# Four layers of attention and feed-forward on one core: key weights held behind a select on GpSimd, and a new hand-written order on every engine

## The chip, the core and the metric

The kernel runs on one NeuronCore of a Trainium2 chip. The metric is the device time of one execution in microseconds (us). The kernel before takes 410.4 us in the median of three runs (410.1 to 411.93).

## What is computed

The reference takes x of 2048 tokens by 512 features (bf16) through four layers: linear attention A, feed-forward B, then A and B again with the same weights. Each layer reads the layernorm of x and adds its result to x.

```
A: q, k, v = layernorm(x) @ wqkv               # 32 heads of 16
   phi(t)  = where(t > 0, t + 1, exp(t)) + 1e-6
   kv = sum over tokens of phi(k)^T v ;  z = sum over tokens of phi(k)
   o  = (phi(q) kv) / (phi(q) z + 1e-6) ;  x = x + o @ wo
B: x = x + (silu(layernorm(x) @ w_gate) * (layernorm(x) @ w_up)) @ w_down   # 1792 wide
```

## The kernel before

**Layout.** The 2048 tokens are 16 tiles of 128, in 4 groups of 4 tiles. x stays in SBUF (`X`) from the first load to the last addition. Layers are numbered 0 to 3; 0 and 2 are attention, 1 and 3 feed-forward. All operations are written into one list; each gets the operations that it depends on, and `sync` (line 64) turns these into semaphore waits. What is not computed by the program is the order: `PROGRAM` (line 169) lists TensorE's products as tokens, and `ORDER` (line 193) gives every other engine (ACT is ScalarE, DVE VectorE, POOL GpSimd, SP SyncE, which only issues transfers) its whole sequence by name, written out. An engine takes its list strictly in that order, so an instruction that waits holds up everything behind it. `ON_ACT` (line 328) chooses an engine for each operation that could run on more than one, and `PE_T` (line 322) names the transposes that TensorE does in place of a transposing transfer.

**Tokens.** The first digit is the layer. `S` is a filler product of zeros (`spin`, line 1229). `t` transposes a tile on TensorE (`xt_pe`, line 614), whose copy out of PSUM is `xT`. `k` and `q` are the key product of a tile and the query product of a group and a quarter of the features (lines 662, 766); each is followed by phi (line 642): `exp` on ACT, on some also `id1` on ACT, then `ts` and `phi` on DVE. `g` adds phi(k)^T x-normalized into four PSUM banks that stay taken for the whole pass. `z` adds the key sums of one tile with four one-column products (line 713); tiles of an attention layer without a `z` token are added by `zs` on DVE or POOL (`z_add`, line 703), and one `s` token (`z_sum`, line 725, with `zh` and `zl` on DVE) brings that sum in. `d` is the denominator, `v` and `m` turn the sums into one 512 by 512 matrix (DVE `mask`, then `evac` by ACT or DVE), `r` repeats 1/den on TensorE, `w` is the output product of a tile, with the residual addition `res` on DVE and the next layer's layernorm (`ln`, line 543: `sq` on ACT, `negm`, `vpe`, `pow`, `nmr` mostly on POOL, `apply` on ACT or DVE, then the transposing transfer `xT` from SP's queue). `u` is a gate and an up product (line 873; two PSUM banks, `silu` or `tanh` on ACT, `h` on DVE). `y` and `p` are the seven half-size products of a Strassen step, for gate and up in layer 3 (`gs`, line 978) and for down (`down`, line 1104).

**1/den.** `den` (line 780) takes 1/den in one of two ways: `ln` and then `rex` on ACT (a logarithm and exponentials of its negative), or `den` on DVE (with a reciprocal) and then `rep`, a plain copy, on ACT. Either makes four repeated tiles, each transposed by a transfer (`rT`) and multiplied in by `pqn` on DVE. Each exponential or logarithm is bound to come before each `silu` of the next feed-forward layer, and the reverse (`after=silus`, `after=exps`).

**Head.** SP issues the loads of x tiles 0, 2, 3, 1 and then pairs of tiles, the query and the value weights. ACT's first two instructions are the loads of the key weights (`ldk`, line 500), which wait for nothing. Tiles 0 and 1 get their mean and variance on DVE (`stats`, `aggr`), tiles 2 and 3 on ACT (`stats`, `sq`); tiles 0 to 3 are transposed on TensorE, 3 copied out by DVE and 0, 1 and 2 by ACT. POOL makes the constants; the block mask (`late_consts`, line 478, three operations) comes last among them. POOL issues the loads of the other weights (`ld`) once all x tiles of layer 0 are transposed.

**PSUM.** `bank` (line 430) gives each product the bank of eight that was touched longest ago in the program's order and isn't pinned.

Of the kernel before, what the change touches and what calls it, by code (L numbers as in the profile page):

```python
# [1350 lines left out]
```

## Time and profile before

| | |
|---|---|
| Runs | 410.4 us median (410.1, 410.4, 411.93) |
| Profiled execution | 410.17 us, of which its span is 408.1 |
| TensorE busy | 398.8 us, 98% of the span |
| VectorE busy | 323.8 us, 79% |
| ScalarE busy | 245.3 us, 60% |
| GpSimd busy | 130.4 us, 32% |
| Chain that ended last | TensorE 93%, VectorE 3%, ScalarE 2%, issue 1%, DMA 1% |
| HBM read, written | 9.70 MB, 2.10 MB |

The span runs from the first to the last instruction; the execution's own time has 2.07 us more around it. The chain is followed back from the last instruction, at each step to what released it. Idle time of an engine off the chain costs nothing by itself. In the rows below "x" is a count; a group's us is busy time, its ns the mean of one; in brackets stands the idle time just before and what ended it. Lines are lines of the kernel.

### The profile page before, as it was taken

To read this page: it belongs to the slowest core of one execution; us is meant where nothing else is said; L and a number is where in the kernel's file an instruction comes from. 1 tells how busy PE (TensorE), PEld (TensorE's weight loads), DVE (VectorE), ACT (ScalarE), POOL (GpSimd) and SP (SyncE) were. 2 spreads that over 40 slices of the span, in tenths; PEclk is the share of its full clock that TensorE was granted. 3 is DMA by queue.
4 is the path that set the end of the run, shared out by engine and by line. 5 is a ranking of instruction groups with operands and counts; after the bars stand their busy time and mean duration, and the time that the engine had idled before them with its cause. 6 is when DMAs were issued, how large, how long until landed. Compare 5 with 4: busy or idle time off the path is not lost.

```text
span 408.1 us, 7644 instructions
## 1 busy us (share of the span) xinstructions
PE 398.8 (98%) x2673; PEld 244.8 (60%) x2714; DVE 323.8 (79%) x754; ACT 245.3 (60%) x492; POOL 130.4 (32%) x277
## 2 busy tenths in 40 slices
PE   7999999999999999999999998999999999999997
PEld 6445544444574764445776444444578778878886
DVE  4996488679558978889787957998588788699796
ACT  5998799654417148344166777897773562576440
POOL 5624137772303015000044210698702142030210
PEclk9999999999999999999999999999999999999999
DMA  8757824932201102000011202434210100100011
GB/s 274 139 104 267 200 51 92 194 54 52 51 2 40 14 2 51 0 1 2 2 26 28 52 2 59 80 58 91 51 27 2 43 11 2 51 2 2 0 53 52
DMA packets 53189, 23.30 MB, mean 57 GB/s; under 512 B 46432, under 2 KB 52064, under 8 KB 53152
## 3 DMA queue, kind: packets, MB, share of 16 engines
q1 hardware_dynamic: 51264, 16.27, 18.9%
q0 software_dynamic: 1344, 6.03, 4.7%
q10 hardware_dynamic: 544, 0.52, 0.4%
q8 instruction: 21, 0.34, 0.4%
q14 instruction: 16, 0.13, 0.1%
HBM read 9.70 MB, written 2.10 MB: 29 GB/s over the span
## 4 chain that ended last, share of the span: by engine, by line
PE 93%; DVE 3%; ACT 2%; issue 1%; DMA 1%; SPq 0%; DVEq 0%; ACTq 0%
PE pb L451 93%; DMA X<-in_A_x_dram 1%; DVE X L865 1%; DVE pq L853 1%; DVE GT L743 0%; ACT xnA L571 0%; ACT xnA L563 0%; DVE pq L835 0%; ACT xnT L630 0%; DVE pq L1212 0%; ACT xnB L598 0%; ACT etmp L571 0%; ACT etmp L646 0%; DVE xnA L1142 0%; DVE xnB L602 0%
## 5 line engine op out<-in xcount | busy, mean ns | idle before, releaser
L451 PE MATMUL pb<-xnT,Wu 128*128 128x512 bf16 (+1 forms) x383 | 95.0, 362 | 0.3
L451 PE MATMUL pb<-xnT,Wg 128*128 128x512 bf16 (+1 forms) x370 | 92.4, 362 | 0.9
L451 PEld LDWEIGHTS pb<-xnT,Wu 128*128 128x128 bf16 x388 | 37.9, 98 | 39.4
L451 PEld LDWEIGHTS pb<-xnT,Wg 128*128 128x128 bf16 x388 | 37.8, 98 | 34.5 <-issue 0.5
L899 DVE TENSOR_TENSOR hT<-tht,pb 128x512 bf16<-128x512 f32 x50 | 34.0, 683 | 21.9 <-PE pb L451 14.8
L897 ACT ACTIVATE tht<-pb 128x512 f32<-128x512 f32 x50 | 29.4, 591 | 27.2 <-PE pb L451 26.5
L646 ACT ACTIVATE etmp<-pb 128x512 bf16<-128x512 f32 x64 | 37.0, 597 | 14.1 <-PE pb L451 11.9
L1025 POOL TENSOR_TENSOR hT<-pq 128x256 bf16<-128x256 f32 x24 | 18.5, 775 | 76.7 <-ACT pq L1015 76.7
L575 POOL TENSOR_SCALAR mv<-sums 128x1 f32<-128x1 f32 x52 | 13.6, 270 | 86.4 <-DVE sums L1222 55.0
L888 ACT ACTIVATE tht<-pb 128x512 f32<-128x512 f32 x32 | 19.0, 595 | 35.5 <-PE pb L451 34.4
L451 PE MATMUL pb<-Wd,hT 128*128 128x256 bf16 x336 | 40.1, 273 | 0.0
L1030 ACT ACTIVATE pq<-pb 128x512 f32<-128x512 f32 x45 | 26.0, 595 | 22.3 <-PE pb L451 19.4
L591 POOL TENSOR_TENSOR rstd<-vpe,negh 128x1 f32<-128x1 f32 x62 | 35.8, 582 | 7.8 <-DVE vpe L587 3.0
L451 PEld LDWEIGHTS pb<-Wd,hT 128*128 128x128 bf16 x336 | 32.9, 98 | 5.7
L1020 DVE TENSOR_TENSOR pq<-pb,pq 128x512 f32<-128x512 f32 x45 | 30.2, 685 | 3.6 <-PE pb L451 1.7
L451 PE MATMUL pb<-Wqkv,xnT 128*128 128x512 bf16 x125 | 30.5, 379 | 1.5 <-ACT xnT L630 1.3
L451 PE MATMUL pb<-GT,pq 128*128 128x512 bf16 x125 | 29.9, 379 | 1.5 <-ACT GT L740 1.4
L451 PE MATMUL pb<-xnT,Wqkv 128*128 128x512 bf16 x122 | 30.9, 379 | 0.3
L451 PE MATMUL pb<-pk,xnA 128*128 128x512 bf16 x123 | 30.7, 378 | 0.3
L651 DVE TENSOR_SCALAR etmp<-etmp 128x512 bf16<-128x512 bf16 x64 | 18.4, 291 | 13.7 <-ACT etmp L646 13.5
L890 DVE SCALAR_TENSOR_TENSOR tht<-tht,pb 128x512 f32<-128x512 f32 x32 | 21.8, 684 | 6.1 <-ACT tht L888 5.9
L571 ACT ACTIVATE etmp<-X,sums 128x512 bf16<-128x512 bf16 x32 | 22.8, 715 | 4.5 <-DVE X L865 4.2
(165 smaller groups left out, 724.6 us busy)
## 6 DMA issues: line engine op xcount, KB each, us to landing
out_dram<-pq SPq DMA_DIRECT2D x16, 128.0 KB, 1.7
Wg<-in_B_w_gate_dram POOLq DMA_DIRECT2D x4, 448.0 KB, 5.1
Wu<-in_B_w_up_dram POOLq DMA_DIRECT2D x4, 448.0 KB, 5.5
Wd<-in_B_w_down_dram POOLq DMA_DIRECT2D x7, 256.0 KB, 4.2
X<-in_A_x_dram SPq DMA_DIRECT2D x6, 256.0 KB, 5.3
Wqkv<-in_A_wqkv_dram SPq DMA_DIRECT2D x2, 512.0 KB, 7.4
X<-in_A_x_dram SPq DMA_DIRECT2D x4, 128.0 KB, 3.5
Wqkv<-in_A_wqkv_dram ACTq DMA_DIRECT2D x2, 256.0 KB, 3.8
```

What stands on the lines that cost most here:

```text
L451: return op("pe", lambda e: e.matmul(o_ap, lhsT=lhsT, rhs=rhs, start=start, stop=stop, skip_group_check=skip), r=r, w=w, n=n)
L571: op("act", lambda a: a.activation(out=sq_ap, in_=X[:, t, :], func=ACT.Square, scale=-float(D), bias=sums[:, t:t + 1], accum_out=mv[:, t, ...
L591: op("pool", lambda p: p.tensor_tensor(out=rstd[:, t:t + 1], in0=vpe[:, t:t + 1], in1=negh[:], op=ALU.pow), r=[f"vp{t}", "negh"], w=[f"rs{ ...
L646: exps.append(op("act", lambda a: a.activation(out=etmp[e][:], in_=PB[pb], func=ACT.Exp), r=[f"pb{pb}"], w=[f"e{e}"], after=silus, kind="e ...
L651: op("dve", lambda v: v.tensor_scalar(out=etmp[e][:], in0=etmp[e][:], scalar1=1.0, scalar2=1e-6, op0=ALU.min, op1=ALU.add), r=[f"e{e}"], w ...
L888: op("act", lambda e: e.activation(out=tht[a][:], in_=PB[pg], func=ACT.Tanh, scale=0.5), r=[f"pb{pg}"], w=[f"th{a}"], kind="tanh")
L890: op("dve", lambda v: v.scalar_tensor_tensor(out=tht[a][:], in0=tht[a][:], scalar=1.0, in1=PB[pg], op0=ALU.add, op1=ALU.mult), r=[f"pb{pg} ...
L897: silus.append(op("act", lambda e: e.activation(out=tht[a][:], in_=PB[pg], func=ACT.Silu), r=[f"pb{pg}"], w=[f"th{a}"], after=exps, kind=" ...
L899: op("dve", lambda v: v.tensor_tensor(out=hT[h][:, j, :], in0=tht[a][:], in1=PB[pu], op=ALU.mult), r=[f"pb{pu}", f"th{a}"], w=hk, kind="h")
L1020: op("dve", lambda v: v.tensor_tensor(out=c, in0=PB[b], in1=c, op=ALU.add), r=[f"pb{b}", k], w=[k], kind="ca")
L1025: lambda e: e.tensor_tensor(out=hT[h][:, jj, o:o + 256], in0=c[:, 0:256], in1=c[:, 256:512], op=ALU.mult),
L1030: op("act", lambda e: e.activation(out=gs_tmp[3 * f + n], in_=PB[pb], func=ACT.Copy), r=pk_, w=[f"gt{3 * f + n}"], kind="cp")
```

## The change

**The wait.** The three mask operations move from `late_consts` ahead of the loads, and both loads of the key weights wait for the second of them, the first select on the mask (`begun`). POOL's order of constants becomes: mask memset, identity memset, 1 + 1e-6, first mask select, identity select, and the rest.

```diff
+        op("pool", lambda g: g.memset(mask[:], 1.0), w=["mask"])
+        begun = op("pool", lambda g: g.affine_select(out=mask3, in_=mask3, compare_op=ALU.is_ge, fill=0.0, base=0,
+                                             pattern=[[-DH, HC], [0, DH]], channel_multiplier=1),
+           r=["mask"], w=["mask"])
...
         for c in range(2):
-            dma("act", Wqkv[:, 2 * c:2 * c + 2, D:2 * D], wq3[:, 2 * c:2 * c + 2, D:2 * D], w=[f"Wk{c}"], kind="ldk")
+            dma("act", Wqkv[:, 2 * c:2 * c + 2, D:2 * D], wq3[:, 2 * c:2 * c + 2, D:2 * D], w=[f"Wk{c}"],
+                after=[begun], kind="ldk")
```

**The order.** All tokens of `PROGRAM` and all lists of `ORDER` are new. In tokens, five `z` of layer 0 go and one `s` comes (so the key sums of tiles 6, 8, 10, 11 and 14 go through `zs`), one transpose on TensorE (`2t1`) takes the place of a transfer, and fillers grow from 54 to 60, of which 52 (before: 51) stand ahead of the first transpose. All other products are the same ones. The head, the end of layer 0 and the passage from layer 2 to layer 3:

```diff
-S S S S S S S S S S S S S S S S S S S S S S S S S S S S S S S S S S S S S S S S S S S S S S S S S S S 0t0 S 0k0 S S
-0t2 0t1 0t3 0k2 0k1 0k3 0q00 0q03 0g0 0g2 0g1 0g3 0k4 0k9 0q01 0k10 0k5 0g4 0z2 0g9 0z1 0k6 0z3 0z10 0q12 0k7 0k13
+S S S S S S S S S S S S S S S S S S S S S S S S S S S S S S S S S S S S S S S S S S S S S S S S S S S S 0t0 S S 0t2 S
+S S S S S 0t1 0k0 0k1 0t3 0k2 0k3 0q00 0g1 0g0 0q03 0g2 0k4 0g3 0k9 0q01 0k5 0k10 0g4 0g9 0k6 0k7 0z2 0z5 0z4 0k13
...
-0v 0q31 0m0 0q33 0m2 0m3 0m1 0w1 0w2 0w3 0d30 0r2 0w0 0w5 0q32 0w4 0d31 0w6 0w7 0w11 0d32 0w9 0w8 0w10 1u000 1u007
+0d13 0d01 0d02 0d12 0d03 0g11 0q10 0q20 0g7 0g10 0d10 0d23 0d11 0g15 0g13 0g12 0d21 0q30 0d22 0d20 0v 0q31 0m1 0m3 0m0
+0m2 0q33 0w1 0w2 0d31 0w3 0d30 0r2 0w0 0q32 0w5 0w6 0w7 0w4 0w10 0w9 0w11 0d32 0w8 0d33 1u008 1u004 1u006 1u001 1u000
...
-2d21 2g15 2q23 2d11 2g1 2q22 2g12 2g6 2d13 2d23 2g8 2g5 2d10 2d12 2g4 2d20 2d22 2q33 2v 2r1 2m3 2m1 2m2 2m0 2w3 2w2
-2w0 2q32 2w1 2w6 2d31 2q30 2w4 2w8 2w7 2d32 2w10 2w9 2d33 2w11 2d30 2w5 3u001 3u010 3u004 3u008 3u005 3u000 3u002
+2d23 2d13 2d20 2g6 2g4 2d22 2g1 2q33 2v 2r1 2m3 2m1 2m0 2m2 2w2 2w3 2w0 2q32 2d33 2w1 2d31 2w6 2w4 2q30 2w8 2d32 2w7
+2w9 2w10 2d30 2w5 2w11 3u010 3u012 3u003 3u004 3u008 3u002 3u007 2w15 3u011 3u005 3u009 2w14 2w12 2w13 3u001 3y101
```

**The lists.** The parts that matter below (ACT at the head, at the end of layer 0 and into layer 3; DVE at the head; POOL around the weight loads; SP at the head):

```diff
-i.ldk i.ldk1 0x2.stats 0x2.sq 0x3.stats 0x3.sq 0t0.xT 0k0.exp 0t2.xT 0t1.xT 0k0.id1 0x4.apply 0k2.exp 0k1.exp 0x6.stats 0k3.exp
+i.ldk i.ldk1 0x2.stats 0x2.sq 0x3.stats 0x3.sq 0t1.xT 0k0.id1 0k0.exp 0k1.exp 0x4.apply 0k2.exp 0x6.stats 0x5.apply
...
-0q20.exp 0q20.id1 0d0.rex2 0d1.ln 0G0.evac 0G2.evac 0G3.evac 0d1.rex1 0q30.exp 0d1.rex 0d2.ln 0d2.rxs 0q31.exp
-0M0.evac 0q33.id1 0M1.evac 0M3.evac 0q33.exp 0d1.rex2 0d1.rex3 1x1.sq 1x2.sq 1x3.sq 1x2.apply 1x0.sq 0q32.id1
+0d0.rex2 0q20.exp 0d1.ln 0d1.rex 0d1.rex1 0G0.evac 0G2.evac 0G3.evac 0d1.rex2 0q30.exp 0d2.ln 0d1.rex3 0d2.rxs
+0q31.exp 0M1.evac 0M0.evac 0M3.evac 0q33.id1 0q33.exp 1x1.sq 1x2.sq 1x3.sq 1x2.apply 0q32.id1 1x0.sq 1x5.sq
...
-2d0.rex2 2d1.ln 2d1.rxs 2G2.evac 2G3.evac 2d2.ln 2q33.exp 2q33.id1 2d2.rex 2d2.rex1 2M1.evac 2M0.evac 2M2.evac
-2d2.rex2 3x3.sq 2d2.rex3 3x2.sq 2q32.exp 3x0.sq 3x1.sq 3x6.sq 2q30.exp 3x0.apply 3x4.sq 3x1.apply 3x7.sq 3x8.sq
-3x10.sq 3x9.sq 3x6.apply 3x4.apply 3u001.silu 2d3.rep1 2d3.rep 3u010.silu 3u004.silu 3x7.apply 3x5.sq 3u008.silu
+2G0.evac 2G2.evac 2G3.evac 2q33.exp 2q33.id1 2d2.rep1 2d2.rep3 2d2.rep 2M1.evac 2M0.evac 2M2.evac 2d2.rep2 3x2.sq
+3x3.sq 2q32.exp 3x0.sq 3x1.sq 3x6.sq 2q30.exp 3x0.apply 3x4.sq 3x1.apply 3x8.sq 2d3.ln 3x7.sq 2d3.rex1 2d3.rex
+3x9.sq 3x5.sq 3x10.sq 3x11.sq 2d3.rex3 2d3.rex2 3u010.silu 3u012.silu 3u003.silu 3x8.apply 3u004.silu 3u008.silu
...
-i.c 0x0.stats 0x0.aggr 0x0.apply 0x1.stats 0x2.vpe 0x1.aggr 0x1.vpe 0x3.vpe 0x2.apply 0x4.stats 0x1.apply 0x3.apply
-0x4.aggr 0x9.stats 0x10.stats 0x9.aggr 0t3.xT 0k0.ts 0x5.stats 0k0.phi 0x9.apply 0x10.aggr 0x5.aggr 0k2.ts
+i.c 0x0.stats 0x2.vpe 0x0.aggr 0x1.stats 0x2.apply 0x1.aggr 0x0.apply 0x1.vpe 0x4.stats 0t0.xT 0x1.apply 0x3.vpe
+0x4.aggr 0t2.xT 0x9.stats 0x3.apply 0x9.aggr 0x10.stats 0x5.stats 0t3.xT 0k0.ts 0x5.aggr 0k1.ts 0k0.phi 0k1.phi
...
-i.c5 i.c i.c2 i.c6 i.c1 i.c4 i.c3 i.c7 i.c8 i.c9 0x0.vpe 0x0.pow 0x2.negm 0x3.negm 0x2.pow 0x1.pow 0x3.pow 0x4.vpe
+i.c7 i.c5 i.c2 i.c8 i.c6 i.c i.c1 i.c4 i.c9 i.c3 0x2.negm 0x2.pow 0x0.vpe 0x0.pow 0x3.negm 0x1.pow 0x3.pow 0x4.vpe
...
+0x7.nmr 0x14.negm 0x15.vpe 0x13.vpe 0x15.pow 0x13.pow 0x14.nmr 0x8.vpe 0x8.pow 0x8.nmr 0k10.zs i.ld 0k14.zs i.ld7
...
-i.ldx i.ldx2 i.ldx3 i.ldx1 i.ldy i.ldy2 i.ldy3 i.ldy1 i.ldq i.ldy5 i.ldy4 i.ldv 0x4.xT 0x9.xT 0x10.xT
+i.ldx2 i.ldx i.ldx1 i.ldx3 i.ldy i.ldy2 i.ldy3 i.ldq i.ldy1 i.ldy4 i.ldy5 i.ldv 0x4.xT 0x9.xT 0x5.xT 0x10.xT 0x6.xT
```

**The engines.** By count of instructions in the lists, ACT goes from 433 to 418, DVE from 690 to 707, POOL from 273 to 264. In layer 0 the copies of tiles 0 and 2 after their transposes go to DVE, one more pair of `rsl` and `rse` to ACT. Into layer 2, `2G0` goes to ACT and the way of 1/den changes in groups 1 and 2 (to DVE and `rep`) and in group 3 (to `ln` and `rex`). In layer 3 eight `apply` go from ACT to DVE.

## Rows read from the trace of the kernel before

**Rows 1.** Windows by stage: length, busy PE, PEld, DVE, ACT, POOL, clock, DMA.
```profile
0.00:8.00 8.00, 5.55 (x56) 5.50 (x58) 2.88 (x10) 4.79 (x10) 3.92 (x20) 1.00 0.80 256
8.00:26.00 18.00, 17.69 (x104) 8.53 (x105) 17.96 (x53) 16.29 (x35) 9.96 (x28) 1.00 0.71 154
...
50.00:62.00 12.00, 11.42 (x92) 5.79 (x92) 10.81 (x29) 11.17 (x26) 3.39 (x10) 1.00 0.33 66
62.00:250.00 188.00, 186.93 (x1099) 104.64 (x1118) 147.75 (x356) 99.42 (x190) 52.42 (x112) 1.00 0.19 38
250.00:264.00 14.00, 12.78 (x97) 6.22 (x98) 13.89 (x37) 12.60 (x28) 6.32 (x18) 1.00 0.31 63
264.00:280.00 16.00, 15.87 (x85) 7.38 (x85) 13.75 (x34) 15.35 (x30) 15.47 (x32) 1.00 0.38 73
...
403.00:409.00 6.00, 2.20 (x21) 1.72 (x18) 2.06 (x6) 0.00 (x0) 0.00 (x0) 0.98 0.26 89
```

**Rows 2.** Timeline of the head: start, duration, engine, what, idle before and releaser.
```profile
0.79 3.82 SPq L494 DMA_DIRECT2D X<-in_A_x_dram  x8
0.82 0.97 ACTq L494 DMA_DIRECT2D Wqkv<-in_A_wqkv_dram  x2
...
1.24 5.28 PE L451 MATMUL pb<-hT 128*128 128x128 bf16 x51 [1.24 <-DVE hT L457]
...
1.85 0.35 POOL L481 TENSOR_SCALAR_AFFINE_SELECT mask<-mask 128x128 bf16<-128x128 bf16 x1
...
4.20 0.63 ACT L563 ACTIVATE xnA<-X 128x512 bf16<-128x512 bf16 x1 [2.13 <-DMA X<-in_A_x_dram]
...
6.31 0.69 DVE L556 BATCH_NORM_STATS2 stats<-X 128x6 f32<-128x512 bf16 x1 [0.92 <-DMA X<-in_A_x_dram]
6.36 0.39 PE L625 MATMUL pb<-ident,xnA 128*128 128x128 bf16 x4
...
8.06 0.81 PE L451 MATMUL pb<-Wqkv,xnT 128*128 128x512 bf16 x3 [1.26 <-ACT xnT L630]
...
10.05 2.12 PE L451 MATMUL pb<-Wqkv,xnT 128*128 128x512 bf16 x9
```

**Rows 3.** The same timeline, later: the first two query products.
```profile
12.65 1.89 PE L451 MATMUL pb<-xnT,Wqkv 128*128 128x512 bf16 x8
```

**Rows 4.** Groups of DVE by line and form over the whole span.
```profile
L556 DVE BATCH_NORM_STATS2 stats<-X 128x6 f32<-128x512 bf16 x12 | 8.1, 681 | 2.8 <-DMA X<-in_A_x_dram 2.8
...
L602 DVE TENSOR_SCALAR xnA<-X,mv,rstd 128x512 bf16<-128x512 bf16 x17 | 6.8, 407 | 2.4 <-POOL rstd L591 2.2
...
L633 DVE COPY xnT<-pb 128x512 bf16<-128x512 bf16 x1 | 0.4, 391 | 0.0
```

**Rows 5.** Timeline of PE in layer 0: a z token and the product after it.
```profile
23.01 0.24 PE L451 MATMUL pb<-ones,pk 128*128 128x1 bf16 x4
23.11 1.02 PE L451 MATMUL pb<-pk,xnA 128*128 128x512 bf16 x4
```

**Rows 6.** Timeline of POOL in layer 0: the first weight load.
```profile
31.44 0.98 POOL L494 DMA_DIRECT2D Wo<-in_A_wo_dram  x1 [4.70 <-DMA xnT<-xnA]
```

**Rows 7.** Timelines of PE and ACT at the end of layer 0.
```profile
55.50 2.60 PE L451 MATMUL pb<-GT,pq 128*128 128x512 bf16 x11 [0.47 <-ACT GT L740]
...
54.84 1.09 ACT L740 ACTIVATE GT<-pb 128x512 bf16<-128x512 f32 x2
```

**Rows 8.** Timelines of PE and ACT in the same place of layer 2.
```profile
255.21 2.75 PE L451 MATMUL pb<-GT,pq 128*128 128x512 bf16 x12 [0.90 <-ACT GT L740]
...
253.98 1.57 ACT L740 ACTIVATE GT<-pb 128x512 bf16<-128x512 f32 x3
```

**Rows 9.** Timelines of PE and ACT where layer 3 begins.
```profile
267.70 1.03 PE L451 MATMUL pb<-xnT,Wg 128*128 128x512 bf16 x4
...
269.58 1.28 ACT L897 ACT_TABLE_LOAD   x1
270.87 0.60 ACT L897 ACTIVATE tht<-pb 128x512 f32<-128x512 f32 x1
```

More of the change, by code (lines that the diff above doesn't have):

```diff
@@ L194 @@
     "act": """
-i.ldk i.ldk1 0x2.stats 0x2.sq 0x3.stats 0x3.sq 0t0.xT 0k0.exp 0t2.xT 0t1.xT 0k0.id1 0x4.apply 0k2.exp 0k1.exp 0x6.stats 0k3.exp
-0q00.id1 0q00.exp 0x5.apply 0q03.exp 0x6.sq 0x14.stats 0x14.sq 0x7.apply 0k4.id1 0k4.exp 0k9.exp 0x14.rsl 0q01.exp
-0x14.rse 0k10.id1 0k10.exp 0k5.exp 0x14.apply 0x11.rsl 0x8.apply 0x11.rse 0k6.exp 0q12.id1 0q12.exp 0k7.id1 0k7.exp
-0k13.exp 0k15.exp 0k13.id1 0k14.exp i.c2 i.c1 0q13.exp i.c3 i.c 0q11.exp 0k8.exp 0k8.id1 0k11.id1 0k11.exp 0q02.exp
-0q02.id1 0q23.id1 0k12.exp 0q23.exp 0q22.id1 0q22.exp 0q21.exp 0d0.ln 0q21.id1 0d0.rex1 0d0.rex 0q10.exp 0d0.rex3
@@ new lines @@
+0q23.exp 0q13.exp 0q22.exp 0q12.id1 0q12.exp 0q02.exp 0q02.id1 0q21.exp 0d0.ln 0d0.rex 0d0.rex1 0d0.rex3 0q10.exp
+0d0.rex2 0q20.exp 0d1.ln 0d1.rex 0d1.rex1 0G0.evac 0G2.evac 0G3.evac 0d1.rex2 0q30.exp 0d2.ln 0d1.rex3 0d2.rxs
+0q31.exp 0M1.evac 0M0.evac 0M3.evac 0q33.id1 0q33.exp 1x1.sq 1x2.sq 1x3.sq 1x2.apply 0q32.id1 1x0.sq 1x5.sq
+0q32.exp 1x6.sq 1x0.apply 1x7.sq 1x4.sq 1x10.sq 1x5.apply 1x9.sq 1x11.sq 1x8.sq 1u008.silu 1u004.silu 0d3.rep
+0d3.rep1 1u006.silu 1u001.silu 1u000.silu 1u005.silu 1u011.silu 1u010.silu 1u012.silu 0d3.rep2 1u009.silu 0d3.rep3
@@ new lines @@
+2q31.exp 2q21.exp 2q13.exp 2q20.exp 2q20.id1 2q22.exp 2d0.ln 2q23.exp 2q23.id1 2d0.rex1 2d0.rex 2d0.rex2 2d0.rex3
+2G0.evac 2G2.evac 2G3.evac 2q33.exp 2q33.id1 2d2.rep1 2d2.rep3 2d2.rep 2M1.evac 2M0.evac 2M2.evac 2d2.rep2 3x2.sq
+3x3.sq 2q32.exp 3x0.sq 3x1.sq 3x6.sq 2q30.exp 3x0.apply 3x4.sq 3x1.apply 3x8.sq 2d3.ln 3x7.sq 2d3.rex1 2d3.rex
+3x9.sq 3x5.sq 3x10.sq 3x11.sq 2d3.rex3 2d3.rex2 3u010.silu 3u012.silu 3u003.silu 3x8.apply 3u004.silu 3u008.silu
+3x7.apply 3u002.silu 3u007.silu 3u011.silu 3x15.sq 3u005.silu 3x5.apply 3u009.silu 3x14.sq 3x12.sq 3x13.sq
@@ L231 @@
+3y333.sih 3y347.cp 3y342.sih 3u313.silu 3y347.sih 3y334.sih 3y344.sih 3y343.sih
 """,
     "dve": """
[L233 to L236 removed]
@@ new lines @@
+0q13.phi 0q22.ts 0q22.phi 0z.zm 0q12.ts 0q12.phi 0q02.ts 0q02.phi 0q21.ts 0q21.phi 0q10.ts 0q10.phi 0q20.ts
+0q20.phi 0d0.pqn 0d0.pqn1 0G1.evac 0d0.pqn2 0d0.pqn3 0v.mask 0q30.ts 0v.mask1 0q30.phi 0d1.pqn 0d2.den 0q31.ts
+0M2.evac 0q31.phi 0d1.pqn2 0d1.pqn1 0w1.res 0q33.ts 0w2.res 0d1.pqn3 0w3.res 0q33.phi 0r2.pqn 1x1.apply 0r2.pqn1
+0w0.res 0r2.pqn2 0w5.res 0r2.pqn3 0w6.res 1x3.apply 0q32.ts 0w7.res 0q32.phi 0w4.res 0w10.res 0w9.res 0w11.res
+1x6.vpe 1x4.vpe 0w8.res 0d3.den 1x6.apply 0d3.den1 1x11.vpe 1x8.vpe 1x7.apply 1u008.h 1u004.h 1u006.h 1x4.apply
```

270 lines of the change are left out of this document (128 added, 142 removed).

## The prediction

> **What bounds the kernel now.** I read the page's busy shares first (the table above has them), then the windows by stage, then PE's waits on the timelines. TensorE is busy 398.8 us of 408.1, at a granted clock of 1.00 in every stage, the 2.4 GHz level. The windows say where most of the other 9.3 us lie [rows 1]: 2.4 in the first 8 us, 0.6 at the end of layer 0, 1.2 between layers 2 and 3, 3.8 after 403 us, and 1.1 in small pieces in the 188 us between. A product of four 512-column steps takes 0.865 us (the two query products of rows 3, eight matmuls in a row, are followed at once). So a new order can win in three places, the head and the two passages through v, m and w, besides what it takes off PE's own work; launch and tail are the same instructions. It can lose wherever it makes PE wait. Idle time that only moves on the other engines costs nothing. "Faster" below means by over 0.5%, 2.05 us, about what a measurement of this kernel can tell from no change.
>
> **Head.** Tiles and key weights are issued in the same microseconds [rows 2]. Tile 2 lets ACT begin only at 4.20, after 2.13 us of waiting, and tile 1 lets DVE go on only at 6.31. PE's first product comes at 8.06, after a wait of 1.26 on ACT's copy of tile 0; PE is full from 10.05, and the first query product starts at 12.65 [rows 2, 3]. I follow the new lists to that product. The select takes 0.35 us [rows 2]; behind two memsets and a constant I put it at 1.3 to 1.65, so the key loads issue at 1.7 in place of 0.82, and ACT is done issuing (0.97) near 2.7. The tiles have the transfers to themselves until then: tile 2, now first, should be there near 3, all four by about 4.5. ACT's two passes over tile 2, of some 0.75 with the read of their sum, end near 4.4. DVE waits for them with tile 2's vpe; from there through the copy of tile 3 it has five stats, four applies, three copies and six small ones. At the 0.34 us that DVE takes per instruction from 8 to 26 us (53 in 17.96 [rows 1]) these 18 take 6.1; by their own means (0.68, 0.41, 0.39 [rows 4], 0.17) they take 7.2, less the overlap of each with the next. I take 6.1, and 0.4 for tile 0's apply, which stands behind two pow's on POOL: 10.9. The last key product follows (0.9), and the first query product starts near 11.9: **0.75 us gained**. By then DVE has also done tile 5's stats, which now come after tile 3's copy, so the pace behind is no worse. The key weights have over 6 us from issue to first use. Ends: if only the first tile came sooner, DVE's part would start 1.1 later, 0.4 lost; if ACT's chain from 4.20 moved by the 1.1 that tile 2 waits now behind another tile, and lost the half of a copy too, 1.5 gained. I take 0.75, the sum by the rows' durations, nearer to the middle. Fillers: 52 stand ahead of the first transpose (51 take 5.28 us [rows 2]), so TensorE reaches it near 6.4 as now, when tile 0's apply is just done; the other eight lie in waits.
>
> The Trainium skill speaks against held loads ("DMA: Bandwidth & Descriptors", Rules for kernel authors): issue a transfer early and wait for it late. By it the first product could come 0.9 us later and the sum would lose that; the first product stands 7.2 us behind the loads' issue now [rows 2], and the sum goes without it.
>
> **PE's own work.** A z token costs the 0.10 us from 23.01 to 23.11 [rows 5]; five go, 0.5. One s token is two such, 0.2; four more transposes at most half of the 0.39 of those now [rows 2], whose last one's latency it includes, 0.2. **0.1 gained.** The key sums go to DVE (three additions, zh, zl) and POOL (two). One queue needs care: on POOL, tile 14's addition stands behind the first weight load, which waits for the last x transpose until 31.44 [rows 6]; tile 8's on DVE waits for it, and DVE's next phi's stand behind that. Key product 8 comes 20 products and four z's after the first query product, at 29.6, its phi near 31.5. I count on the transposes landing some 2.5 us sooner (0.7 from the head, the rest because tile 6's apply moves up in DVE's list) and take nothing. Else POOL's addition, longer than its load's 0.98, ends near 33.6, DVE stands 2 us, and PE, with three free banks, about 1: 0 to 1.0 lost.
>
> **End of layer 0.** Now one query product lies between the m products and two copies of ACT behind an id1, so PE waits 0.47 before 55.50 and ACT's last copy ends at 55.93 [rows 7]. In the new order the four m come first, the query product covers the copies, and ACT does them in a row. ACT ends the third some 5.25 us after the last g; PE wants it, for the fourth step of the first w, after 5.45. **0.4 gained**; ends 0.5 gained, 0.1 lost.
>
> **End of layer 2.** Here ACT's list ahead of the three M copies gets longer: three G copies, exp, id1 and three rep, in place of ln, rxs, two G copies, ln, exp, id1 and two rex. The third G copy replaces the three short ones; the third rep adds 0.5, as long as a copy (three in 1.57 [rows 8]); the G copies start a little sooner. **0.3 lost** on a wait that is now 0.90 [rows 8]; ends 0.2 gained, 0.7 lost.
>
> **Into layer 3.** Now ACT loads silu's table at 269.58 and does the first silu at 270.87, 3.2 us after the first u product starts [rows 9]; 1/den of group 3 needs no exponential and comes later. In the new order its ln and four rex must precede the first silu, and the squares of tiles 5 and 11 do too. Added: 0.35, 4 x 0.52 and 2 x 0.75, 3.9; taken away: two applies, 1.5; and PE comes to the first u one w (0.87) sooner after the query product whose exp opens this part of ACT's list. So the first silu starts 3.2 + 3.9 - 1.5 + 0.9 = 6.5 us after the first u, ends at 7.1 and frees a bank. A u takes 1.73 us and two of eight banks, so PE runs four, 6.9 us, before it needs that bank. **0.4 lost** (0.2 here, 0.2 because tile 1's transpose lands about as the first u begins). The last two rex also wait until the transposes have read the first two tiles. Ends: 0, and 2.0 lost if that takes 2 us longer than the squares between hide.
>
> The Trainium skill ("ScalarE: Activation LUTs", What ACT_TABLE_LOAD costs) puts a switch of tables at a load of 1.28 us and a drain of 1.38 behind it. The row has silu 0.01 us after the load's end [rows 9]. With the page, the first silu would come 1.4 later and the time would be 411.2; I go by the row.
>
> **Between and tail.** Layers 1 and 3 keep their products; PE waits for next to nothing there now, and DVE, busy 148 of 188 us [rows 1], has room for 17 more instructions, eight applies among them. The down product 23 now lies between the last y and the last group's first down product and covers the last sums: **0.1 gained**; ends 0.3 gained, 0.1 lost.
>
> **Sum** against the profiled execution of 410.17: -0.75 - 0.1 - 0.4 + 0.3 + 0.4 - 0.1 = -0.65, so 409.5. The median of the runs is 0.23 above that execution: the forecast is **409.8**.
>
> **Rivals.**
> 1. *Everything is covered, faster.* The head at its end (1.5), the end of layer 0 too (0.5), nothing lost at the first silu, 0.4 of layer 2's 0.90 gained, 0.2 in PE and tail: -2.6, 407.8. For it: the head's waits of 2.13, 0.92 and 1.26 are real [rows 2]. Against it: DVE is busy 17.96 of 18 us from 8 to 26 [rows 1] and must pass on what ACT wins. Chance 0.19.
> 2. *The first silu is late, slower.* It stands behind rex3 and rex2, those behind two transposes of SP, those behind the transposes of tiles 0 to 3. From 6.9 us after the first u each further microsecond stops PE for one. At 10 us PE stands 3.1 instead of 0.2: 412.7. For it: ACT is busy 15.35 of 16 us in that stretch [rows 1] and can't catch up. Against it: PE has four u in hand. Chance 0.12.
> 3. *The held load changes nothing.* The head is set by DVE's own work, wherever the tiles land: it gives 0, the rest +0.1: 410.5. Chance 0.11.
> 4. The forecast, 0.58.
>
> **Numbers.** Cases 3 and 4 lie within 0.5% (408.35 to 412.45); what the forecast spreads over the edges and what the other two spread inside cancel. Faster 0.19, same 0.69, slower 0.12. The ends summed would be wider than any likely outcome; the range reaches past case 1 and most of the way to case 2, 407.6 to 412.2.
>
> **What would show it.** Right: ACT's first pass over a tile near 3 us, the first query product near 11.9, 20 fewer columns of z, no wait before the first w of layer 0, one of 1.2 in layer 2, the first silu 6 to 7 us after the first u and a wait of a few tenths at the fifth. Wrong: tiles landing as late as now, DVE standing at tile 8's addition, PE waiting over a microsecond anywhere between 62 and 400 us, or any stretch with PE's clock under 1.00.

## The result: 413.93 us, slower by 0.8%

The kernel after takes 413.93 us in the median of 7 runs (412.39 to 416.12), against 410.2 before (7 runs, 410.1 to 411.93). The ratio is 1.0082, 95% interval [1.0063, 1.0102]. The forecast was 409.8 with a range up to 412.2: the sign was wrong, and the result lies outside.

The profiled execution took 415.59 us (span 413.8). First the windows of after; columns as in [rows 1].

```profile
0.00:8.00 8.00, 6.45 (x68) 6.11 (x68) 2.78 (x9) 3.61 (x8) 3.17 (x19) 1.00 0.71 217
8.00:26.00 18.00, 16.24 (x73) 7.37 (x76) 16.13 (x48) 14.75 (x32) 10.61 (x27) 0.91 0.61 160
...
50.00:62.00 12.00, 11.62 (x96) 5.79 (x96) 9.28 (x26) 9.68 (x22) 1.41 (x5) 1.00 0.59 80
62.00:250.00 188.00, 186.01 (x1086) 104.11 (x1105) 149.06 (x357) 98.34 (x187) 55.62 (x117) 1.00 0.18 35
250.00:264.00 14.00, 12.18 (x103) 6.19 (x104) 12.02 (x30) 10.88 (x23) 1.79 (x7) 1.00 0.38 76
264.00:280.00 16.00, 14.85 (x79) 6.66 (x77) 14.55 (x44) 15.08 (x34) 14.84 (x32) 1.00 0.37 75
```

TensorE is idle 1.76 us from 8 to 26 (0.31 in [rows 1]), 1.99 from 62 to 250 (1.07), 1.82 from 250 to 264 (1.22) and 1.15 from 264 to 280 (0.13). From 8 to 26 its granted clock is 0.91. Now the timeline of TensorE in the head (start, duration, engine, what, idle before and releaser), against [rows 2, 3]:

```profile
7.46 0.50 PE L450 MATMUL pb<-hT 128*128 128x128 bf16 x6
9.49 0.60 PE L625 MATMUL pb<-ident,xnA 128*128 128x128 bf16 x4 [1.52 <-DVE vpe L587]
10.31 2.98 PE L450 MATMUL pb<-Wqkv,xnT 128*128 128x512 bf16 x7 [0.22 <-issue]
...
15.08 1.03 PE L450 MATMUL pb<-xnT,Wqkv 128*128 128x512 bf16 x4
```

The first key product comes at 10.31 in place of 8.06, the first query product at 15.08 in place of 12.65. TensorE waits 1.52 us for tile 1's apply (the row names vpe, the next on VectorE), and then seven products take 2.98 us. The granted clock, in windows of 1 us, says why:

```profile
9.00:10.00 1.00, 0.51 (x4) 0.52 (x6) 1.00 (x6) 0.00 (x0) 0.43 (x1) 0.77 1.09 364
10.00:11.00 1.00, 0.78 (x3) 0.34 (x3) 1.00 (x4) 0.60 (x1) 0.83 (x3) 0.50 1.10 350
11.00:12.00 1.00, 1.00 (x3) 0.30 (x2) 1.00 (x2) 0.17 (x1) 0.82 (x4) 0.50 1.09 350
12.00:13.00 1.00, 1.00 (x4) 0.44 (x3) 0.07 (x1) 1.00 (x2) 0.36 (x1) 0.52 1.09 347
```

0.50 is the 1.2 GHz level. VectorE's timeline shows what tile 1's apply (the L602 row) stood behind:

```profile
8.09 0.69 DVE L556 BATCH_NORM_STATS2 stats<-X 128x6 f32<-128x512 bf16 x1 [1.19 <-DMA X<-in_A_x_dram]
8.70 0.41 DVE L633 COPY xnT<-pb 128x512 bf16<-128x512 bf16 x1
9.03 0.40 DVE L602 TENSOR_SCALAR xnA<-X,mv,rstd 128x512 bf16<-128x512 bf16 x1
```

VectorE waits 1.19 us for tile 4, whose pair lands at 8.07 in place of 7.04; tile 0's copy and tile 1's apply are behind that in its list. The end of layer 2 and the start of layer 3 on TensorE, against [rows 8, 9]:

```profile
259.43 2.75 PE L450 MATMUL pb<-GT,pq 128*128 128x512 bf16 x12 [1.11 <-ACT GT L740]
...
273.11 1.02 PE L450 MATMUL pb<-xnT,Wg 128*128 128x512 bf16 x4 [1.03 <-issue]
```

The first u of layer 3 waits 1.03 us where it waited about nothing. ScalarE at the start of layer 3, where the forecast had feared for the first silu:

```profile
276.43 1.28 ACT L897 ACT_TABLE_LOAD   x1
277.72 1.57 ACT L897 ACTIVATE tht<-pb 128x512 f32<-128x512 f32 x3
```

The first silu comes 4.6 us after the first u, and the fifth u (280.01) waits for nothing.

For the experiments I use these starts of TensorE's first weight load of each kind, in the profiled execution of each kernel (us; "after 2" is the kernel after once more, experiment 5):

| | before | after | after 2 | a_two | a_rep |
|---|---|---|---|---|---|
| first query product | 12.43 | 14.86 | 13.01 | 12.36 | 12.11 |
| v of layer 0 | 51.14 | 53.42 | 51.92 | 51.16 | 51.01 |
| first w of layer 0 | 54.43 | 57.63 | 55.80 | 54.77 | 54.62 |
| first u of layer 1 | 67.41 | 70.72 | 68.86 | 67.64 | 67.63 |
| v of layer 2 | 251.40 | 255.11 | 253.22 | 251.99 | 251.98 |
| first w of layer 2 | 255.18 | 259.40 | 258.87 | 256.00 | 256.00 |
| first u of layer 3 | 267.50 | 273.08 | 272.40 | 268.64 | 269.88 |

A first weight load can stand ahead of a wait inside its own product. In layer 0 it does so in before: the second step of the first w starts only at 55.50, behind the wait of [rows 7]. In after and a_two it follows at once:

```profile
57.64 1.90 PE L450 MATMUL pb<-GT,pq 128*128 128x512 bf16 x8
```

```profile
54.77 1.90 PE L445 MATMUL pb<-GT,pq 128*128 128x512 bf16 x8
```

So in layer 0 "v to the first w" below compares kernels of one order with each other. Across the two orders the second step compares: 4.36 us after v in before, 4.44 in after, 3.84 in a_two and in a_rep.

### The profile page after: what moved, and what is told of

It reads as the page before. It is cut to its first block, busy times and chain, and to the rows that moved or that the text cites. A ratio compares the mean times of both kernels' runs of the same rounds, so it can differ in the third digit from the quotient of the medians.

```text
span 413.8 us, 7648 instructions
## 1 busy us (share of the span) xinstructions
PE 401.1 (97%) x2672; PEld 245.6 (59%) x2712; DVE 332.7 (80%) x771; ACT 237.5 (57%) x477; POOL 131.1 (32%) x268
## 4 chain that ended last, share of the span: by engine, by line
PE 90%; ACT 4%; DMA 3%; issue 2%; DVE 0%; SPq 0%; ACTq 0%
PE pb L450 90%; DMA X<-in_A_x_dram 1%; DMA RT<-rrep 1%; ACT GT L740 1%; ACT etmp L646 1%; ACT pk L649 0%; ACT esel L488 0%; SPq L493 0%; ACT rrep L817 0%; PE pb L625 0%; DVE stats L556 0%; ACT pq L649 0%; ACT rrep L822 0%; ACT hT L822 0%; DVE pq L1212 0%
## 5 line engine op out<-in xcount | busy, mean ns | idle before, releaser
L899 DVE TENSOR_TENSOR hT<-tht,pb 128x512 bf16<-128x512 f32 x53 | 35.7, 683 | 18.3 <-PE pb L450 17.4
L1025 POOL TENSOR_TENSOR hT<-pq 128x256 bf16<-128x256 f32 x23 | 17.3, 761 | 75.1 <-ACT pq L1015 75.0
L450 PE MATMUL pb<-xnT,Wqkv 128*128 128x512 bf16 x124 | 31.8, 379 | 0.4
L651 DVE TENSOR_SCALAR etmp<-etmp 128x512 bf16<-128x512 bf16 x64 | 20.1, 319 | 9.2 <-ACT etmp L646 9.0
L1015 ACT ACTIVATE pq<-pq 128x256 f32<-128x256 f32 x45 | 18.4, 414 | 11.1 <-DVE pq L1020 10.9
```

What stands on the lines that cost most here:

```text
L450: return op("pe", lambda e: e.matmul(o_ap, lhsT=lhsT, rhs=rhs, start=start, stop=stop, skip_group_check=skip), r=r, w=w, n=n)
L651: op("dve", lambda v: v.tensor_scalar(out=etmp[e][:], in0=etmp[e][:], scalar1=1.0, scalar2=1e-6, op0=ALU.min, op1=ALU.add), r=[f"e{e}"], w ...
L899: op("dve", lambda v: v.tensor_tensor(out=hT[h][:, j, :], in0=tht[a][:], in1=PB[pu], op=ALU.mult), r=[f"pb{pu}", f"th{a}"], w=hk, kind="h")
L1015: silus.append(op("act", lambda e: e.activation(out=o_ap, in_=i_ap, func=ACT.Silu), r=r, w=w, after=exps, kind="sih"))
L1025: lambda e: e.tensor_tensor(out=hT[h][:, jj, o:o + 256], in0=c[:, 0:256], in1=c[:, 256:512], op=ALU.mult),
```

## The experiments

My theory after reading the two traces was **A**: about 2 us are lost in the head because the held load delays the whole stream, and about 3 in small waits of the new order behind it. Rivals: **B**, the new order alone; **C**, the held load alone. Of the kernels below, those named a_ start from the kernel after, b_ from before, h_ are halves of both.

**1 to 4. Halves, and the wait by itself.** h_head has before's lists and placements (no wait) up to v of layer 0 and after's from there; h_tail has after's up to v of layer 2 and before's from there. In the other two:

```diff
 b_hold = before, with
+POOL: i.c7 i.c5 i.c2 i.c8 i.c6 i.c i.c1 i.c4 i.c9 i.c3 ...
+dma("act", Wqkv[...], ..., after=[begun], kind="ldk")
 a_free = after, with
-dma("act", Wqkv[...], ..., after=[begun], kind="ldk")
+dma("act", Wqkv[...], ..., kind="ldk")
```

h_head: 

> The lists and placements of the kernel before, without the wait, up to and including v of layer 0, and those of the kernel after from there on. Theory A (the loss has a part in the head, about 2.1 us of the profiled 5.4 by the first w of layer 0, and a part behind it, in small waits before the first u of layers 1 and 3 and around m of layer 2): the head's part comes back, 411.5 to 412.3 us. Theory B (the head is harmless, the new order of layers 1 to 3 costs everything): 413 to 414. Theory C (the held load alone costs everything): 410 to 410.8.

h_tail: 

> The kernel after, wait and all, up to and including v of layer 2, and the lists and placements of the kernel before from there on. Theory A: the passage of m and w of layer 2 (0.4) and the wait before the first u of layer 3 (1.0 to 1.2) go away, the head's loss and layer 1's stay: 412.2 to 412.9 us. Theory B: 411 to 412, half of its loss lies there. Theory C: no change against the kernel after, 413.5 to 414.2.

b_hold: 

> The kernel before with the wait alone: GpSimd's first constants in the order of the kernel after, Wk's two loads behind the first select, all lists else as before. Theory A: the whole stream of loads moves by about 1 us and VectorE's list passes on what the late pair of tiles 4 and 5 brings: 411.0 to 412.0 us, first key product 1 us or more later. Theory B: within 0.4 of the kernel before, 409.8 to 410.6. Theory C: 413 to 414.

a_free: 

> The kernel after without the wait: Wk's loads are issued at once, everything else as in the kernel after. Theory A: the loads land about 1 us sooner, VectorE's list no longer waits for tile 4, the engine's clock stays up in the head: 411.8 to 412.9 us. Theory B: 413.3 to 414.2, no change against the kernel after. Theory C: 410 to 410.8.

Measured, with before at 410.28 beside them: h_head 414.0 (ratio 1.0103 [1.0073, 1.0133]), h_tail 412.54 (1.0068 [1.0043, 1.0092]), b_hold 410.44 (1.0006 [0.9995, 1.0017]), a_free 412.25 (1.006 [1.0034, 1.0085]). The wait alone costs the old order nothing that can be told from noise (0.7 us at most by its interval), so C falls. With before's head the loss is all there, so A's size for the head falls; but h_head is no clean measure, since its seam lies in the passage of layer 0, and from v to the first u it takes 18.22 us where before takes 16.27 and after 17.30. In h_tail, whose head is that of after with the wait, the first query product comes at 12.40 and the clock stays up: what the profiled execution of after lost there it doesn't lose in every run.

a_free's profile showed where else time goes. TensorE in the passage of layer 2, and then the granted clock in windows of 1 us:

```profile
254.43 1.04 PE L450 MATMUL pb<-Wo,KVT 128*128 128x512 bf16 x4 [0.40 <-DVE KVT L754]
258.06 4.22 PE L450 MATMUL pb<-GT,pq 128*128 128x512 bf16 x11 [2.59 <-ACT GT L740]
```

```profile
257.00:258.00 1.00, 0.00 (x0) 0.00 (x0) 0.63 (x2) 1.00 (x3) 0.00 (x0) 1.00 0.00 0
258.00:259.00 1.00, 0.94 (x3) 0.38 (x4) 0.00 (x0) 0.92 (x2) 0.00 (x0) 0.58 0.65 131
259.00:260.00 1.00, 1.00 (x4) 0.29 (x2) 0.11 (x1) 0.00 (x0) 0.00 (x0) 0.50 0.51 100
```

The first w waits 2.59 us for m's evictions (`evac`, the copies out of PSUM), and the clock falls to 0.50 behind that. Neither A, B nor C says this, so I formed **D**: the new order costs 2.4 to 3.1 us in places that every run shows, and stretches at half clock add to some runs. Rivals: **A'**, the held load costs 2 us in the head in every run; **E**, the wait before layer 3 has another source than the one named; **F**, the passage of layer 2 is not set by these lists.

**5 to 8. After again, and single instructions moved.**

```diff
 a_same = after, unchanged
 a_two = after, with
-POOL: ... 3x1.pow gsw.ws2 3x1.nmr ...
+POOL: ... 3x1.pow 3x1.nmr gsw.ws2 ...
-ACT:  ... 2d2.rep1 2d2.rep3 2d2.rep 2M1.evac 2M0.evac 2M2.evac 2d2.rep2 ...
+ACT:  ... 2d2.rep1 2d2.rep3 2M1.evac 2M0.evac 2M2.evac 2d2.rep 2d2.rep2 ...
 b_ws = before, with
-POOL: ... 3x1.pow 3x6.vpe 3x1.nmr 3x4.negm 3x6.pow 3x6.negm gsw.ws ...
+POOL: ... 3x1.pow 3x6.vpe gsw.ws 3x1.nmr 3x4.negm 3x6.pow 3x6.negm ...
 b_m = before, with
+ACT:  2d2.rex1 behind 2M2.evac; 3x1.apply ahead of 3x4.sq
+DVE:  gsw.ws7 behind 2r1.pqn3
+POOL: 3x6.vpe behind 3x1.nmr
```

a_same: 

> The kernel after once more, unchanged. Theory D (formed on the first four runs: the new order of layers 1 to 3 costs 2.4 to 3.1 us in places that every run shows, and short stretches at half clock add 1.7 to 3 in some runs): 412.4 to 413.2 where the clock stays at full, with the first query product near 12.4 us and v of layer 0 near 51 as in the kernel before; about 1 run in 3 above 414. Theory A' (the held load costs 2 us in the head in every run): first query product near 14.9, every run above 413.

a_two: 

> The kernel after with two instructions moved: GpSimd's third weight sum of layer 3's first group behind tile 1's nmr instead of ahead of it, and ScalarE's third replica of layer 2's third group behind the three evictions of m instead of ahead of them. Theory D: from the first w of layer 2 to the first u of layer 3 12.4 to 12.7 us instead of 13.7, from v to the first w of layer 2 3.8 instead of 4.2 to 4.3, together 1.3 to 1.7 us less than the kernel after in the same job. Rival E (another of the four x transposes or the tile's own square is late by as much): the first stretch stays above 13.4 us.

b_ws: 

> The kernel before with one instruction moved on GpSimd: the first weight sum of layer 3, 1.15 us there, goes ahead of tile 1's nmr. Theory D: tile 1's apply and its transpose, the fourth that the first u of layer 3 waits for, land 1.0 to 1.3 us later, and the time rises by as much, 411.2 to 411.6 us. Rival E (the wait before the first u comes from elsewhere): 410.0 to 410.5.

b_m: 

> The kernel before with the passage of layer 2 shortened: ScalarE's second replica behind the three evictions of m, one weight sum of VectorE behind the fourth product of group 1's replicas, tile 6's vpe on GpSimd behind tile 1's nmr, and tile 1's apply on ScalarE ahead of tile 4's square. Theory D (the stage's waits are set by the order of these lists): from v to the first w of layer 2 3.3 instead of 3.8 us, the first u of layer 3 0.2 to 0.5 us sooner, 409.7 to 410.1 us. Rival F (something else ends last there, such as the transposes of the replicas): no change, 410.1 to 410.4, or a loss.

Measured, with before at 410.22: a_same 414.08 (7 runs, 412.11 to 415.99; 1.0088 [1.006, 1.0116]), a_two 412.34 (6 runs, 410.93 to 413.32; 1.0038 [1.0016, 1.0059]), b_ws 410.81 (ratio 1.0012 [1.0, 1.0024]), b_m 410.62 (0.9999 [0.9983, 1.0015]).

*Layer 3.* From the first w of layer 2 to the first u of layer 3: before 12.32 us, after 13.68, a_same 13.53, a_two 12.64, b_ws 13.13. So one weight sum on GpSimd, put between tile 1's pow and its nmr, makes most of that wait, in either kernel; E falls by the traces. In time b_ws lies between the two: 410.81, where D expected 411.2 to 411.6 and E at most 410.5. GpSimd in after, in a_two (its lines are numbered 5 lower) and in b_ws:

```profile
266.79 0.56 POOL L591 TENSOR_TENSOR rstd<-vpe,negh 128x1 f32<-128x1 f32 x1
267.32 1.32 POOL L956 TENSOR_TENSOR Wqkv<-Wu 128x512 bf16<-128x512 bf16 x1
268.63 0.29 POOL L595 TENSOR_SCALAR nmr<-mv,rstd 128x1 f32<-128x1 f32 x1
```

```profile
263.56 0.56 POOL L586 TENSOR_TENSOR rstd<-vpe,negh 128x1 f32<-128x1 f32 x1
264.23 0.43 POOL L590 TENSOR_SCALAR nmr<-mv,rstd 128x1 f32<-128x1 f32 x1
264.63 1.15 POOL L951 TENSOR_TENSOR Wqkv<-Wu 128x512 bf16<-128x512 bf16 x1
```

```profile
264.97 1.22 POOL L952 TENSOR_TENSOR Wqkv<-Wg 128x512 bf16<-128x512 bf16 x1
266.18 0.26 POOL L591 TENSOR_SCALAR nmr<-mv,rstd 128x1 f32<-128x1 f32 x1
```

nmr is what tile 1's apply on ScalarE needs, the apply releases the fourth x transpose, and the first u needs all four.

What a_two wins ahead of the first u it can lose behind it. From there to the end its profiled execution takes 138.60 us, where after and a_same take 137.50. VectorE and TensorE in a_two:

```profile
279.20 0.52 DVE L830 TENSOR_TENSOR pq<-pq,RT 128x512 bf16<-128x512 bf16 x1 [2.88 <-DMA RT<-rrep]
```

```profile
280.97 1.04 PE L445 MATMUL pb<-xnT,Wu 128*128 128x512 bf16 x4 [0.92 <-DVE hT L894]
```

The transpose of a replica of group 3 (one of the four repeated tiles of 1/den) lands 3.20 us after its issue ended, VectorE's list has its product ahead of the next h, and a u waits for that h. In a_three and a_two_free (below) the same transpose takes 2.79 and 2.91 us and the stretch 138.58 and 138.22; in a_two_again, a_all, a_four and a_four_free it takes 1.28 or 1.29, and the stretch 137.50 to 137.51.

*Layer 2.* ScalarE and TensorE in a_same, where v to the first w takes 5.65 us at full clock:

```profile
257.15 0.63 ACT L822 ACTIVATE rrep<-rtok 128x512 bf16<-128x512 bf16 x1 [1.24 <-DMA RT<-rrep]
257.69 1.55 ACT L740 ACTIVATE GT<-pb 128x512 bf16<-128x512 f32 x3
```

```profile
258.90 2.75 PE L450 MATMUL pb<-GT,pq 128*128 128x512 bf16 x12 [2.46 <-ACT GT L740]
```

This is the third replica of group 2. It overwrites `rrep`, which the transpose of group 0's replica still reads; that transpose was issued from 252.74 and landed at 257.13, 3.1 us after its issue ended, where most take 1.24. m's evictions are behind the replica in ScalarE's list, so TensorE waits for that landing. In a_free the same transpose is late (3.3 us, landing at 256.29), the replica starts at 256.31. In before it lands at 247.66, and the replica that needs its buffer first starts near 253: no landing there could reach the evictions. In a_two the replica is behind them:

```profile
254.81 1.57 ACT L735 ACTIVATE GT<-pb 128x512 bf16<-128x512 f32 x3
256.25 0.64 ACT L817 ACTIVATE rrep<-rtok 128x512 bf16<-128x512 bf16 x1
```

v to the first w: before 3.78, after 4.29, a_two 4.01 (D had expected 3.8). b_m, which moves one of before's, gains nothing (3.77): with one replica fewer ahead of them, the evictions start at the same time, when m is there. F holds for before: its order wasn't the limit, and it is not improved this way.

That left **G**: replicas stand ahead of m's evictions on ScalarE, in layer 2 and in layer 0, and wait there for transposes that land late in some runs. Rivals: **H**, the slowest runs have another source; **I**, the passage of layer 0 is set by another engine.

**9 to 12. One instruction, three places, and the converse.**

```diff
 a_rep = after, with
+ACT:  2d2.rep behind 2M2.evac
 a_three = a_two, with
+ACT:  0d1.rex2 0d1.rex3 behind 0M3.evac
 a_all = a_three without the wait of the key loads
 b_d0 = before, with
-ACT:  ... 0d1.rex 0d2.ln 0d2.rxs 0q31.exp 0M0.evac ... 0q33.exp 0d1.rex2 0d1.rex3 ...
+ACT:  ... 0d1.rex 0d1.rex2 0d2.ln 0d1.rex3 0d2.rxs 0q31.exp 0M0.evac ... 0q33.exp ...
```

a_rep: 

> The kernel after with one instruction moved: ScalarE's third replica of layer 2's third group, which writes the buffer that a transpose of group 0's replicas still reads, goes behind the three evictions of m. Theory G (formed on the first eight runs: replicas stand ahead of m's evictions on ScalarE and wait there for transposes that land up to 2 us late in some runs): the slow tail goes, no run above 414, lowest 411.8 to 412.1, median 412.4 to 413.0. Rival H (the tail comes from the held load or from layer 0): still about 4 runs in 10 above 414.

a_three: 

> The kernel after with three places mended: the third replica behind m's evictions in layer 2, the weight sum behind tile 1's nmr on GpSimd, and in layer 0 the third and fourth replicas of group 1 behind m's evictions on ScalarE as in the kernel before. Theory G: v of layer 0 to its first w 3.2 to 3.4 us instead of 3.6 to 4.2, median 411.2 to 411.9. Rival I (the layer 0 passage is set by the order on TensorE or VectorE): 3.6 us stays, median 411.9 to 412.5.

a_all: 

> The same three places mended, and Wk's loads no longer held. Theory G with a price of 0 to 0.3 us for the held load: 411.0 to 411.6, at most 0.3 below the kernel with the three places alone. Rival A (the held load costs about 1 us in this order): 410.2 to 410.8.

b_d0: 

> The kernel before with two instructions moved: in layer 0 the third and fourth replicas of group 1 go ahead of m's evictions on ScalarE, as in the kernel after. Theory G: the evictions start about 1 us later, v to the first w 3.9 to 4.4 us instead of 3.3, the time 410.7 to 411.2. Rival I: no change, 410.0 to 410.4.

Measured, with before at 410.3: a_rep 412.3 (6 runs, 412.07 to 413.85; 1.0043 [1.0026, 1.006]), a_three 414.97 (5 runs, 414.62 to 416.07), a_all 414.19 (6 runs, 413.94 to 415.16), b_d0 410.99 (12 runs, 410.77 to 412.33; 1.0015 [1.0005, 1.0025]).

a_rep is as G has it: of the 14 runs of after and a_same 7 took over 414 us, of these 6 none, and none of the 36 of a_two, a_two_again, a_two_free, a_four and a_four_free. H keeps a part: 3 of the 9 runs of h_tail took over 414, and its list, too, has that replica behind m's evictions. The profiled execution of after is a case of H, since its 415.59 us come with that transpose in time (1.22 us) and the fall of the clock in the head. a_all is the sharper test of the mechanism, since in its profiled execution the same transpose landed as late as in a_same (3.16 us after its issue, at 258.92), and v to the first w took 4.01 us all the same. Its TensorE there:

```profile
259.04 1.24 PE L445 MATMUL pb<-GT,pq 128*128 128x512 bf16 x5 [0.83 <-ACT GT L735]
```

b_d0 shows that two replicas ahead of m's evictions cost before 0.7 us (0.2 to 1.0 by the interval): v to the first w 4.12 instead of 3.29. But the converse in after, a_three, failed: slower by more than 2 us. ScalarE's replicas came later, and VectorE, whose list in after takes their product ahead of the first residual addition, stood still from 56.58 to 59.30 for the transpose of the third (landed at 59.27); the first u of layer 1 slid to 71.69. So this run didn't price the passage.

**13 to 16. What stayed open:** whether the held load costs the new order anything, the passage of layer 0 with both engines' lists changed, and whether the named places are the whole loss. **J**: it costs a little in most runs; **K**: nothing.

```diff
 a_two_again = a_two
 a_two_free = a_two without the wait of the key loads
 a_four = a_two, with
+ACT:  0d1.rex2 0d1.rex3 behind 0q33.exp
+DVE:  0d1.pqn2 behind 0r2.pqn; 0d1.pqn3 behind 0r2.pqn1
 a_four_free = a_four without the wait of the key loads
```

a_two_again: 

> The kernel after with the third replica of layer 2 behind m's evictions and the weight sum behind tile 1's nmr, once more, beside the three others of this job: 411.0 to 413.3 us as before, median near 412.

a_two_free: 

> The same without the wait on Wk's loads. Theory J (in the new order the held load makes the head's end vary by some tenths to 2 us from run to run, but costs little in most): median 0.2 to 0.8 us below the same kernel with the wait, and its runs closer together. Rival K (in the new order the held load costs nothing, as it did in the old one): within 0.2 us of it.

a_four: 

> The same two places mended, with the wait, and layer 0's passage on both engines: the third and fourth replicas of group 1 behind query product 33's exp on ScalarE as in the kernel before, and the two products that use them on VectorE behind the first and second of group 2's. Theory G (what stands ahead of m's evictions on ScalarE sets the first w): v to the first w 3.2 to 3.4 us instead of 3.6, the first u of layer 1 0.2 to 0.4 us sooner, the median 0.2 to 0.5 below the kernel with two places. Rival I (other engines set the first w): no change.

a_four_free: 

> All three places mended and the wait gone, the rest of the new order as it is. If those four are the whole loss: 410.0 to 410.8 us, the kernel before's time within 0.4; if something else of the new order costs too: 411 or more.

Measured, with before at 410.14: a_two_again 411.96 (6 runs, 411.02 to 412.58; 1.0035 [1.002, 1.0051]), a_two_free 411.09 (12 runs, 410.81 to 412.56; 1.0026 [1.0014, 1.0038]), a_four 412.16 (6 runs, 411.32 to 412.96), a_four_free 412.17 (6 runs, 411.68 to 413.47). With the wait the median is 0.9 us higher in the first pair, 0.8 in the pair of a_three and a_all, 1.7 in that of after and a_free, the same in the pair of a_four, and 0.2 higher in the old order. In each pair of the new order the intervals of the two ratios overlap, so the direction is J's, and no price of the wait is shown. The profiled executions of the first pair do not show it in the head: v of layer 0 comes at 51.19 with the wait and at 51.27 without.

a_four gains nothing at the first w (3.60 us after v, as a_two's 3.61), and from there to the first u of layer 1 it takes 13.72 us, as a_four_free does, where a_two takes 12.87. So rival I holds: the two replicas are not what sets that passage in the new order, and the change on VectorE made it longer. a_four_free at 412.17, well above its expected 410.8, says that the named places are not the whole loss.

One more place shows in the traces. In layer 0 the new order also has two replicas of group 1 ahead of the evictions `0G0`, `0G2` and `0G3`, which v needs (before has them behind). ScalarE and TensorE in after:

```profile
51.53 1.15 ACT L817 ACTIVATE rrep<-dsb 128x512 bf16<-128x512 f32 x2 [1.27 <-DMA RT<-rrep]
52.59 1.55 ACT L740 ACTIVATE GT<-pb 128x512 bf16<-128x512 f32 x3
```

```profile
54.19 0.90 PE L450 MATMUL pb<-GT,Wqkv 128*128 128x128 bf16 x13 [0.26 <-ACT GT L740]
```

They wait for a transpose of group 0 that lands 3.93 us after its issue, and v then waits for these evictions. Its products span 1.08 us in a_two and 1.67 in after, and v to the first w is 0.6 longer there. The same goes for a_same, a_free, a_three and a_four_free, whose v spans 1.35 to 1.88 us. This is the mechanism of theory G, one passage earlier; it is read from the traces, and no run moved these two. No version here beats before.

## Why the prediction was wrong, step by step

The largest misses first. The third replica of layer 2, priced at its duration of 0.5, made its passage 1.87 us longer in a_same, and moving it alone brought the median from 413.9 to 412.3 (the ratio from 1.0082 to 1.0043). Tile 1's nmr, which the sum passed over, cost 1.2 in a_same. The tiles that were to land "all four by about 4.5" landed up to 7.16, and 0.75 gained at the first query product became 0.6 lost in a_same and 2.4 in after.

**Head, -0.75 forecast.** The step that failed is "all four by about 4.5". In the 9 profiles with the wait the fourth tile lands at 6.21 to 7.16 us, in the 9 without it at 5.76 to 6.29; the pair of tiles 4 and 5 at 7.00 to 8.07 against 6.47 to 7.04. With the wait the first three tiles land early (2.97, 3.36 and 5.20 in after; 3.08, 4.18 and 5.70 before) and what follows lands late. The select and tile 2 came as forecast: the key loads issue at 1.59, and ScalarE's first pass starts at 2.99. I had followed VectorE's instructions up to tile 3's copy and not asked when tile 4, whose stats stand among them, would land. In a_rep, with the wait and at full clock, that copy ends at 11.31 against 11.12 in before, and the first query product comes at 12.11: 0.3 gained, the most of any kernel with the wait (a_free, without it, has 12.06). In after the pair was at its latest, TensorE waited 1.52 us, the clock fell, and 2.4 were lost. My low end, 0.4 lost, had no case with a fall of the clock.

The Trainium skill ("DMA: Bandwidth & Descriptors", Rules for kernel authors) had spoken against holding a load: issue early, wait late. The pairs here point the same way in the new order (0.8, 0.9 and 1.7 lost in three, 0 in one), none of them clear of noise, and show no price in the old one (b_hold).

**PE's own work, -0.1.** As small as forecast: TensorE is busy 398.92 us in a_same, at full clock, against 398.76. The queue for which I had bounded a loss cost nothing: in a_same POOL's addition for tile 14 ends at 34.20, before VectorE's phi of tile 8 (ends at 35.16).

**End of layer 0, -0.4.** The mechanism was right at the first w: it comes without a wait of its own (57.64 in after, straight behind the query product), and its second step is 0.5 us sooner after v than in before wherever v is not stretched (3.84 in a_two and a_rep, 4.36 in before). In after the late transpose ahead of v's evictions took that back (4.44). But what counts is the first u of layer 1, which waits in both kernels for the fourth x transpose (67.25 in before, 67.47 in a_two), not for the w's. From v to that u: before 16.27, a_two 16.48, a_rep 16.62, after 17.30. So 0.2 to 1.0 lost. The step that failed is taking the passage up to the first w. VectorE's new list shows where a_two's half microsecond can have gone: the residual additions of tiles 5 and 6 now stand ahead of tile 3's apply, which starts 12.01 us after v in place of 11.83, though the first residual starts 0.5 sooner. No run moved them.

**End of layer 2, +0.3.** Right in mechanism and size where the transpose is in time: 0.51 between the profiled executions of before and after, 0.23 once the third replica is moved. Wrong in its ends (0.2 gained, 0.7 lost): I priced the replica's duration and not the buffer that it writes. When the transpose that reads it is late, the loss is 1.9 (a_same).

**Into layer 3, +0.4.** In after the first silu, from which I took the term and rival 2, hides: it comes 4.6 us after the first u, not 6.5, since the first u itself came late while ScalarE worked on. The transpose of tile 1, worth 0.2 to me, was the whole term: 1.36 in after. I had followed ScalarE's list and SP's and passed over GpSimd's, where a weight sum of 1.32 us was set ahead of tile 1's nmr. Moving it gives back 0.9 to 1.2 up to the first u (12.64 in a_two against 13.68 in after, 13.53 in a_same, 13.88 in a_rep); the rest, 0.3, was not traced. In the time no gain shows: a_rep without that move has 412.3, a_two with it 412.34 and 411.96. In a_two, a_two_free and a_three 0.7 to 1.1 us are lost again behind the first u, at the product with group 3's replicas, which the forecast had not followed on VectorE. Rival 2's 412.7 was the nearest of the cases to the result, but by luck: it had TensorE stop for the first silu, and in after TensorE never did.

On the table load, row and page differ as they did before: silu starts 0.01 us after the load's end (276.43 plus 1.28, silu at 277.72), where the Trainium skill ("ScalarE: Activation LUTs", What ACT_TABLE_LOAD costs) puts a drain of 1.38.

**Between and tail, -0.1.** From the first u of layer 3 to the end 137.50 us in after and a_same against 137.70: 0.2 gained, as forecast. From the first u of layer 1 to v of layer 2 184.39 against 183.99: 0.4 lost, which I had at nothing here. Of this 0.2 are the four transposes of `2t1` (148.76 to 148.98 in a_two), which I had counted under PE's own work; where the rest goes is open. The clock, which I had at 1.00 in every stage of before, is 0.98 in the last [rows 1].

The terms add up on a_same, the kernel after at full clock: 0.78 to v, 0.67 to the first u of layer 1, 0.37 to v of layer 2, 1.87 to its first w, 1.21 to the first u of layer 3, -0.2 behind it: 4.7, and its last product ends 4.7 later than before's (409.90 against 405.20). With the head level (0.78 less) and that passage as in after (4.29 in place of 5.65) it would be 2.6: 414.70, the time of that execution, less 2.1 is 412.6, among the lower runs of the kernel after (412.11 to 413.16).
